# A planned attention and feed-forward kernel: later due times for some transfers, one operation that may change its engine, and the order drawn up anew

## The chip, the core and the metric

The kernel runs on one core of a Trainium2 chip. The core has TensorE (matrix products, results in PSUM), VectorE, ScalarE and GpSimd (elementwise work), and SyncE, which here issues every transfer. The engines run side by side, each through its own queue in order, and wait for one another by semaphores. The metric is the device time of one execution in microseconds (us); the median of several executions is compared. In the profile the engines are PE (matmuls), PEld (TensorE's weight loads), DVE (VectorE), ACT (ScalarE), POOL (GpSimd) and SP (SyncE); a q behind the name is the engine's sequencer.

## What is computed

```python
def _attn_ref(q, k, v):                      # (4, 8, 576, 64) each
    scores = scale * np.matmul(q, k.transpose(0, 1, 3, 2))
    mask = block_i >= block_j                # blocks of 64 positions
    scores = np.where(mask, scores, -1000000000.0)
    scores = scores - np.max(scores, axis=-1, keepdims=True)
    attn = np.exp(scores)
    attn = attn / (np.sum(attn, axis=-1, keepdims=True) + 1e-09)
    return np.matmul(attn, v)

def _moe_ref(x, w1, w2, w3, w_out):          # x: 2304 tokens x 512; w1, w2 512 x 1024, w3 1024 x 1024
    a = x @ w1
    b = x @ w2
    h = a * b @ w3
    return h @ w_out

def _moe2_ref(x, w_in, w_out):               # 512 x 2048, 2048 x 512
    h = x @ w_in
    g = np.where(h > 0.0, h, np.exp(np.minimum(h, 0.0)) - 1.0)
    return g @ w_out

# attention, then _moe_ref, then _moe2_ref
```

The weights arrive as 64-bit words, which the kernel turns into 32-bit floats on the chip.

## The kernel before

**Stages.** Attention is done for 16 pairs of heads (`attention`, n = 0 to 15). For a pair, q and k are loaded (lines 555; the first pair, `whole`, in two pieces each at line 550), copied to the matmul type by ScalarE with their remainders on GpSimd and VectorE (lines 591 to 604), then scores, row maxima on VectorE (lines 681, 748, 807), exponents on ScalarE (lines 686, 759, 819), transposes and the product with v (line 860). Beside the first pairs, weight blocks of 128 x 512 are converted (`convert`) and w3 is multiplied with w_out (`w_product`), so that the first feed-forward part needs one product less. `block2` runs that part over six blocks of 384 tokens, and the last stage (`part_h`, `part_o`) the second part, both with each operand split in two and three products per pair. In the second half of `block2`'s time the weights of the last stage are converted and combined (`t_unit`) and stored in DRAM, from which the last stage reads them again.

**A conversion.** `convert` issues a 512 KB load (line 471), then two ScalarE steps on the loaded words: `c0` (line 439, or on VectorE, line 441), which writes a `ct` buffer, and `c1` (line 432); VectorE steps `c2` to `c4` (lines 445, 448, 453), and the addition `c5` on GpSimd (lines 459, 462). The first conversions take turns in four raw slots (`raw64`, which lie in space that attention results use later) and three `ct` buffers. `w_product` ends with a copy on ScalarE and a subtraction on VectorE (lines 948, 951), which free its PSUM bank.

**Normalising.** When a pair's exponent sums are there, GpSimd adds them up (lines 893, 894), VectorE takes reciprocals (lines 886, 888), SyncE stores them to a scratch tensor in DRAM (line 901, four transfers) and fetches them back broadcast over partitions (line 909, three transfers of 144, 128 and 16 KB). Then GpSimd multiplies the pair's results with them in place (`norm`, line 921, 128 x 576). `block2` reads the results of four pairs.

**The order of work** is made by a planner when the kernel is built. `Plan.add` (line 196) takes each operation with an engine, an estimated duration, what it reads and writes, a priority, other engines it may run on (`ways`) and a `lag`. `Plan.run` (line 233) goes through estimated time: it takes the engine that can start an operation first and, of the operations that can start then, that of the lowest priority number, and emits it. So each engine's queue is fixed at build time. A transfer is estimated in lines 270 to 274: 1.8 us, its bytes at 300 GB/s behind the transfers before it, and 0.05 and 0.3 us; at most eight are in flight. An operation whose inputs end at a time is ready a little later (lines 286 and 287): by `SEEN` of its engine and by its own `lag`. Before the first product of `w_product` the planner also emits spare matmuls (line 1603) where it expects TensorE to be idle, so that TensorE doesn't stand still. `TURNS` (line 59) replaces the priority of single operations, by their number; it holds 520 entries.

```python
        o.prio = TURNS.get(o.n, o.prio)
...
                pipe = max(pipe, t + 1.8) + o.nbytes / 300e3 + 0.05
                o.end, free[e] = pipe + 0.3, t + 0.5
...
                    late = 0.0 if "GATE" in (e, u.eng) else self.SEEN[next(iter(u.ways))] + u.lag
                u.ready = max(u.ready, o.end + late)
```

Of the kernel before, what the change touches and what calls it, by code (L numbers as in the profile page):

```python
# [23 lines left out]
LAG = 0.1  # L24
NLEAD = 2
# [34 lines left out]
    5: -2499.99, 16: -2398.97, 29: -2498.05, 32: -2398.96, 47: -2398.96, 49: -2398.97, 51: -10090.89, 65: -2470.26,  # L60
    73: -2499.48, 83: -2499.91, 84: -9969.15, 90: -2499.99, 96: -2382.01, 99: -2536.18, 100: -10090.93, 105: -2486.89,
    110: -9965.2, 117: -2499.38, 118: -979.78, 120: -2495.46, 123: -2499.17, 138: -2499.41, 141: -2479.33,
    150: -2499.07, 157: -2497.98, 160: -2497.99, 164: -10051.79, 168: -10049.44, 169: -976.72, 173: -2498.88,
    177: -2497.99, 208: -2499.16, 210: -10117.81, 222: 40.01, 232: -10117.85, 248: -2546.58, 265: -2499.27,
    267: -2500.0, 273: -2498.28, 279: -2499.95, 281: -2494.99, 282: -2493.99, 286: -2498.69, 289: -10035.15,
    309: -2536.17, 313: -998.01, 333: -2491.66, 353: -10093.41, 358: -2493.99, 359: -2398.97, 363: -10093.4,
    370: -10025.68, 372: -10202.0, 379: -2498.88, 384: -10049.47, 385: -10117.8, 386: -10117.82, 387: -10117.84,
    394: -980.72, 401: -10074.7, 403: -9811.57, 411: -2393.99, 427: -10207.76, 444: -9971.65, 445: -9934.45,
    468: -991.98, 481: -2393.01, 503: -2435.46, 504: -2396.5, 505: -2394.01, 509: 10010.01, 525: -8999.99,
    532: -992.01, 533: -10066.53, 559: -991.99, 607: -991.99, 613: 44.01, 616: 45.97, 634: 46.01, 653: 54.01,  # L70
    672: -10024.51, 677: -2393.02, 678: -9000.03, 686: -2384.98, 689: -10000.01, 697: 42.02, 699: -2384.99,
    713: 79.99, 720: 498.18, 731: -10019.6, 744: -9928.04, 748: -9928.03, 755: -9881.69, 761: -9881.69, 763: 53.97,
    766: -10044.21, 768: -10008.85, 785: -2499.98, 803: 66.01, 804: -10001.91, 808: 65.99, 818: -10076.0, 819: 63.98,
    821: 64.51, 822: -10000.02, 823: 67.01, 848: 490.13, 876: -10272.6, 883: -10272.61, 887: -10160.95,
    889: -10160.94, 896: -10160.99, 898: -10160.96, 915: 8.35, 936: 118.77, 942: -10161.0, 951: 10121.63,
    954: -9963.56, 961: 509.01, 975: 112.01, 986: -10161.03, 989: 132.33, 997: -10176.58, 1004: -10176.57,
    1008: -10176.56, 1009: 104.0, 1011: -10161.05, 1014: -10018.92, 1017: -10189.77, 1019: -10161.02, 1024: -10176.6,
    1052: -9998.99, 1055: -10231.87, 1061: -10176.62, 1063: -10127.57, 1072: -10231.88, 1073: 152.94, 1078: 82.42,
    1088: 103.97, 1090: 103.97, 1116: 155.74, 1126: 184.21, 1136: -10017.39, 1147: -10017.4, 1154: -10176.62,
    1174: 55.0, 1175: -987.59, 1181: 54.99, 1184: 528.98, 1185: 101.83, 1194: -10022.9, 1203: 71.99, 1206: -10047.65,  # L80
    1209: 19.03, 1213: 505.99, 1218: 72.08, 1220: -10070.02, 1221: 505.01, 1225: -9968.26, 1232: 70.01,
    1233: -9875.34, 1240: 511.0, 1242: -9980.39, 1243: 84.99, 1274: -10032.31, 1275: 129.99, 1283: 132.0,
    1284: -9999.01, 1296: -10176.63, 1298: 156.1, 1347: 136.02, 1348: -9990.74, 1349: 126.99, 1357: 136.02,
    1360: 153.29, 1361: 151.47, 1369: -10157.37, 1371: -9880.0, 1407: 144.01, 1416: 142.1, 1424: 135.97,
    1429: -9999.02, 1431: 11456.16, 1433: 143.99, 1440: 135.94, 1442: 143.98, 1480: 155.01, 1484: -10069.46,
    1486: -10069.47, 1497: 151.99, 1498: 151.99, 1531: -10014.96, 1533: -10014.95, 1542: 10040.01, 1556: 10019.98,
    1557: 52.11, 1558: 10080.65, 1562: -9985.61, 1563: -10008.86, 1567: 61.96, 1569: 538.43, 1579: 10050.01,
    1586: 63.99, 1587: -10272.57, 1593: 65.96, 1595: -10161.02, 1596: -10160.96, 1601: 51.99, 1602: -9947.44,
    1606: -9881.7, 1607: -9985.6, 1608: 79.99, 1609: -9985.59, 1614: 10075.01, 1615: 65.98, 1628: -10160.99,
    1630: -10147.07, 1631: -10161.01, 1632: -10161.02, 1648: 505.02, 1650: -10047.64, 1655: -10161.01,  # L90
    1657: -10160.96, 1665: 92.12, 1666: -10176.57, 1670: -10176.57, 1673: -10176.57, 1674: -10176.58, 1679: 103.98,
    1680: 103.97, 1693: 109.38, 1694: -9789.98, 1695: -10176.63, 1698: -10176.59, 1699: -10176.61, 1701: -10176.6,
    1706: -10185.48, 1707: -10211.42, 1714: 11404.99, 1715: -9871.01, 1726: 142.4, 1727: 145.99, 1730: -9834.31,
    1731: 11410.02, 1732: 132.01, 1734: 103.93, 1738: 134.51, 1739: 125.98, 1741: 125.99, 1750: 144.02,
    1755: 12662.72, 1761: 12705.01, 1774: 100.86, 1780: 148.04, 1782: 143.99, 1783: 135.95, 1810: 12734.98,
# [1565 lines left out]
```

## Time and profile before

| | us |
|---|---|
| median of 3 runs | 903.3 |
| lowest and highest | 900.35, 904.62 |
| profiled execution, whole time | 904.66 |
| its span, first to last instruction | 902.9 |
| TensorE busy (matmuls) | 882.3 |
| VectorE, GpSimd, ScalarE busy | 720.0, 566.3, 505.0 |

The profile is of one execution. Its span is the time from the first to the last instruction; the whole time is 1.8 us longer. Busy means that an instruction of the engine is in flight. Matmuls overlap in TensorE's pipeline, so its busy time counts no time twice but says nothing on how full the pipeline is; its granted clock was 1.00 of full speed. A wait is put down to the instruction or transfer that came last before the waiting one began.

### The profile page before, as it was taken

Reading aid. Unit: us, or ns where it says so; the run is one execution under the profiler, and the core shown is the slowest. Engines: PE = TensorE matmul, PEld = TensorE weight load, DVE = VectorE, ACT = ScalarE, POOL = GpSimd, SP = SyncE. Lnnn points to the kernel's source line nnn. Section 1 sums busy time; section 2 is a strip of 40 time slices with the busy share of each in tenths; the row PEclk is TensorE's granted clock in tenths of the full one; section 3 lists DMA queues with packets and bytes.
Section 4 is the critical chain, followed back from the end, with each engine's and each line's share of the span. In section 5 each row is a group of like instructions: output and inputs, shape, how many; then the busy total and the mean of one; then the engine's idle time right before and its main releaser. Section 6 shows DMA issues by size and latency. Waiting matters only on the chain.

```text
span 902.9 us, 15289 instructions
## 1 busy us (share of the span) xinstructions
PE 882.3 (98%) x5233; PEld 784.3 (87%) x5233; DVE 720.0 (80%) x1349; ACT 505.0 (56%) x1151; POOL 566.3 (63%) x570
## 2 busy tenths in 40 slices
PE   8998999999999999999999999999999999999998
PEld 4544479787878789999999999999999999999998
DVE  6988898877656666668888887879897688887896
ACT  6866587776566654336354554446545465544461
POOL 3676677665423236579888884137876378951786
PEclk9999999999999999999999999999999999999999
DMA  6767643556422106777475967777589776788656
GB/s 223 234 174 226 204 142 108 162 162 190 139 78 77 58 15 225 227 238 254 163 246 198 313 202 250 249 233 250 206 285 309 252 264 208 237 325 276 227 185 232
DMA packets 101037, 186.14 MB, mean 206 GB/s; under 512 B 8544, under 2 KB 51040, under 8 KB 100960
## 3 DMA queue, kind: packets, MB, share of 16 engines
q1 hardware_dynamic: 100960, 185.18, 62.2%
q8 instruction: 41, 0.67, 0.3%
q14 instruction: 36, 0.29, 0.1%
HBM read 147.85 MB, written 37.30 MB: 205 GB/s over the span
## 4 chain that ended last, share of the span: by engine, by line
PE 74%; DVE 11%; DMA 7%; ACT 3%; POOL 3%; issue 2%; SPq 0%; POOLq 0%; DVEq 0%; ACTq 0%
PE y L1012 10%; PE b L1051 10%; PE a L1051 10%; PE hx L1302 7%; PE ox L1381 6%; PE oz L1381 5%; PE hz L1302 5%; PE hy L1302 4%; PE o L860 4%; PE oy L1381 3%; PE t L697 2%; DMA cr<-w 2%; PE s L658 2%; DMA out<-ob 2%; DVE ct L445 1%
## 5 line engine op out<-in xcount | busy, mean ns | idle before, releaser
L1012 PE MATMUL y<-g,slab_lo 128*128 128x384 f32 x576 | 114.9, 340 | 1.7 <-DVE xy L1035 1.0
L1051 PE MATMUL a<-xs,slab_lo 128*128 128x384 f32 x576 | 111.3, 337 | 0.0
L1051 PE MATMUL b<-xs,slab_lo 128*128 128x384 f32 x576 | 111.1, 337 | 0.0
L1012 PEld LDWEIGHTS y<-g,slab_lo 128*128 128x128 f32 x576 | 99.1, 188 | 4.5 <-DVE xy L1035 2.0
L1051 PEld LDWEIGHTS b<-xs,slab_lo 128*128 128x128 f32 x576 | 100.0, 188 | 0.9 <-DVE slab_lo L951 0.7
L1051 PEld LDWEIGHTS a<-xs,slab_lo 128*128 128x128 f32 x576 | 100.0, 188 | 0.9 <-DVE ct L453 0.4
L1302 PE MATMUL hx<-sy,win 128*128 128x384 f32 x432 | 86.6, 336 | 0.6 <-DVE ga L1184 0.5
L1302 PEld LDWEIGHTS hx<-sy,win 128*128 128x128 f32 x432 | 75.5, 188 | 2.2 <-DVE ga L1184 1.5
L1381 PE MATMUL ox<-sp,wout 128*128 128x384 f32 x372 | 74.2, 334 | 0.0
L973 POOL TENSOR_TENSOR g<-af,g 128x384 fp32r<-128x384 f32 x48 | 55.0, 1149 | 29.8 <-ACT g L970 29.3
L1381 PEld LDWEIGHTS ox<-sp,wout 128*128 128x128 f32 x372 | 65.4, 188 | 0.0
L937 PE MATMUL wps<-full,full 128*128 128x512 f32 x128 | 59.9, 602 | 3.2 <-POOL full L462 2.0
L439 ACT ACTIVATE ct<-cr 128x512 f32<-128x512 f32 x61 | 41.3, 677 | 33.2 <-POOL wt L462 16.0
L1302 PE MATMUL hz<-sy,win 128*128 128x384 f32 x288 | 58.1, 336 | 0.3
L1302 PE MATMUL hy<-sy,win 128*128 128x384 f32 x288 | 57.6, 335 | 0.8 <-DVE ga L1184 0.8
L432 ACT ACTIVATE cr<-cr 128x512 int32<-128x512 uint32 x72 | 48.8, 681 | 16.0 <-DMA cr<-w 9.0
L1175 POOL TENSOR_TENSOR sp<-ga,sp 128x384 fp32r<-128x384 f32 x23 | 25.3, 1107 | 49.8 <-ACT sp L1174 37.9
L860 PEld LDWEIGHTS o<-pt,v 128*64 128x64 f32 (+1 forms) x448 | 27.8, 135 | 31.8 <-issue 6.8
L860 PE MATMUL o<-pt,v 128*64 128x320 f32 (+4 forms) x448 | 52.7, 367 | 2.7 <-ACT pt L528 2.3
L921 POOL TENSOR_TENSOR xy<-xy,rr 128x576 f32<-128x576 f32 x16 | 23.3, 1454 | 48.6 <-DMA rr<-scr 29.9
L1381 PE MATMUL oz<-sp,wout 128*128 128x384 f32 x264 | 51.8, 336 | 1.4 <-DVE cp L1184 1.2
L459 POOL TENSOR_TENSOR ct<-ct,cr 128x512 int32<-128x512 int32 x28 | 39.9, 1426 | 20.5 <-DVE ct L453 10.8
(194 smaller groups left out, 2228.1 us busy)
## 6 DMA issues: line engine op xcount, KB each, us to landing
wout<-wso SPq DMA_DIRECT2D x84, 512.0 KB
cr<-w SPq DMA_DIRECT2D x48, 512.0 KB
win<-wsi SPq DMA_DIRECT2D x24, 1024.0 KB
win<-wsi SPq DMA_DIRECT2D x24, 768.0 KB
cr<-w3T SPq DMA_DIRECT2D x16, 512.0 KB
wsi<-wh SPq DMA_DIRECT2D x8, 896.0 KB
wsi<-wt SPq DMA_DIRECT2D x8, 896.0 KB
wso<-wh SPq DMA_DIRECT2D x8, 896.0 KB
```

The lines of the kernel that those rows point to most:

```text
L432: nc.scalar.activation(out=low, in_=low.bitcast(U32), func=AF.Copy, scale=2.0**-29)
L439: nc.scalar.activation(out=t().bitcast(F32), in_=words()[1].bitcast(F32), func=AF.Abs)
L459: nc.gpsimd.tensor_tensor(out=t(), in0=t(), in1=words()[0], op=ALU.add)
L860: nc.tensor.matmul(o()[D * h:D * h + D, lo:cols], lhsT=vt()[0:kn, j, D * h:D * h + D], rhs=p, start=(j == 0), stop=(j == last),)
L921: nc.gpsimd.tensor_tensor(out=a, in0=a, in1=rr(), op=ALU.mult)
L937: nc.tensor.matmul(ps(), lhsT=a[:, j, :], rhs=bb, start=(j == 0), stop=(j == KF - 1))
L973: lambda: nc.gpsimd.tensor_tensor(out=g()[:, 1, :], in0=src(), in1=g()[:, 0, :].bitcast(F32), op=ALU.subtract),
L1012: nc.tensor.matmul(ps()[:, 0:T2], lhsT=w[:, a, n * P:(n + 1) * P], rhs=gs[m]()[:, c, :], start=(m == ms[0] and q == 0), stop=(m == ms[-1] ...
L1051: nc.tensor.matmul(ps()[:, 0:T2], lhsT=w[:, a, u, k, :], rhs=xs()[:, k, c, :], start=(k == 0 and q == 0), stop=(k == KD - 1 and q == 2),)
L1175: lo = lambda eng: eng.tensor_tensor(out=dst(1), in0=src(), in1=dst(0).bitcast(F32), op=ALU.subtract)
L1302: nc.tensor.matmul(bk()[:, 0:T3], lhsT=w[:, a, k, :], rhs=s_(c), start=(first and k == 0 and i == 0), stop=(k == 1 and i == 2), skip_group ...
L1381: nc.tensor.matmul(to[n]()[:, 0:T3], lhsT=w[:, a, n * P:(n + 1) * P], rhs=sp(c), start=(first and q == 0 and i == 0), stop=(q == KP - 1 an ...
```

## The change

`LOADED` (0.5 us) becomes the `lag` of the two ScalarE steps of a conversion that read the loaded words, and of the ScalarE copies of q and k for all pairs but the first; the scaling of the first pair's k gets a lag of 0.7, and the normalisation one of `FETCH` (1.6 us). The normalisation may also run on VectorE, at an estimate of 0.76 us against 1.4 on GpSimd. `TURNS` is replaced: 447 entries stand where 520 stood, 146 operations have one in both, four of them with the same value. No operation is added or taken away, and no buffer changes.

```diff
 LAG = 0.1
+LOADED = 0.5
+FETCH = 1.6
...
 TURNS = {
-    5: -2499.99, 16: -2398.97, 29: -2498.05, 32: -2398.96, 47: -2398.96, 49: -2398.97, 51: -10090.89, 65: -2470.26,
...
+    5: -2499.99, 16: -2329.56, 17: -2495.99, 29: -2498.01, 32: -2329.57, 33: -10133.18, 35: -2499.98, 41: -2499.99,
...
         add(
-            "ACT", 0.68, lambda: c0(nc.scalar), r=[rk], w=[t], prio=prio,
+            "ACT", 0.68, lambda: c0(nc.scalar), r=[rk], w=[t], prio=prio, lag=LOADED,
             ways=[("DVE", 0.42, lambda: c0(nc.vector), True)],
         )
-        add("ACT", 0.68, c1, r=[rk], w=[rk2], prio=prio)
+        add("ACT", 0.68, c1, r=[rk], w=[rk2], prio=prio, lag=LOADED)
...
-                    "ACT", act_us(cn, True), lambda cs=cs: scale_k(nc.scalar, cs), r=[(ks, 0, c)], w=[(ks, 1, c)], prio=pr,
+                    "ACT", act_us(cn, True), lambda cs=cs: scale_k(nc.scalar, cs), r=[(ks, 0, c)], w=[(ks, 1, c)], prio=pr, lag=0.7,
...
-            add("ACT", 0.67, lambda: nc.scalar.copy(qs()[:, 0, :], raw()[:, 0, :]), r=[(raw, 0)], w=[(qs, 0)], prio=pr)
+            add("ACT", 0.67, lambda: nc.scalar.copy(qs()[:, 0, :], raw()[:, 0, :]), r=[(raw, 0)], w=[(qs, 0)], prio=pr, lag=LOADED)
...
-                r=[(raw, 1)], w=[(ks, 0)], prio=pr,
+                r=[(raw, 1)], w=[(ks, 0)], prio=pr, lag=LOADED,
...
-        def norm():
+        def norm(eng):
             a = xy[b]()[:, hp, :]
-            nc.gpsimd.tensor_tensor(out=a, in0=a, in1=rr(), op=ALU.mult)
+            eng.tensor_tensor(out=a, in0=a, in1=rr(), op=ALU.mult)
 
         add(
-            "POOL", 1.4, norm, r=[(rr, 0, 0), (rr, 1, 0), (rr, 1, 1), *((xy[b], hp, c) for c in range(2))],
-            w=[(xy[b], hp, "n"), *((xy[b], hp, c) for c in range(2))], prio=pr, port=True,
+            "POOL", 1.4, lambda: norm(nc.gpsimd), r=[(rr, 0, 0), (rr, 1, 0), (rr, 1, 1), *((xy[b], hp, c) for c in range(2))],
+            w=[(xy[b], hp, "n"), *((xy[b], hp, c) for c in range(2))], prio=pr, port=True, lag=FETCH,
+            ways=[("DVE", 0.76, lambda: norm(nc.vector), True)],
         )
```

## Rows read from the trace of the kernel before

**Rows 1.** The page's busy table: us busy, share of span, instructions

```profile
PE 882.3 (98%) x5233; PEld 784.3 (87%) x5233; DVE 720.0 (80%) x1349; ACT 505.0 (56%) x1151; POOL 566.3 (63%) x570
```

**Rows 2.** TensorE's timeline, start: start us, us, engine, line, out<-in, count [idle before]

```profile
1.96 2.31 PE L1603 MATMUL spare<-mk 128*128 128x512 bf16 x5 [1.96 <-POOL mk L1449]
```

**Rows 3.** Timeline of the end, TensorE's last matmuls

```profile
894.93 4.33 PE L1381 MATMUL oy<-sx,wout 128*128 128x384 f32 x24
```

**Rows 4.** Busy us by stretch: stretch, length, each engine (instructions), clock, DMA share, GB/s

```profile
core 0: us, PE busy (x) PEld busy (x) DVE busy (x) ACT busy (x) POOL busy (x), PEclk, DMA share, GB/s
0.00:125.00 125.00, 113.58 (x540) 60.44 (x540) 106.58 (x208) 85.44 (x199) 76.51 (x93) 1.00 0.66 208
125.00:350.00 225.00, 223.30 (x1583) 185.62 (x1584) 162.15 (x429) 147.12 (x406) 111.66 (x133) 1.00 0.36 115
350.00:850.00 500.00, 496.92 (x2838) 490.59 (x2837) 409.54 (x655) 250.00 (x500) 335.99 (x309) 1.00 0.74 247
```

**Rows 5.** TensorE's timeline, 0 to 125 us: matmuls that waited

```profile
51.29 0.87 PE L697 MATMUL t<-ident,p 128*128 128x128 f32 x6 [1.18 <-ACT p L686]
...
68.31 0.44 PE L770 MATMUL t<-ident,p 128*128 128x128 f32 x2 [1.04 <-DVE pt L529]
...
76.17 0.87 PE L860 MATMUL o<-pt,v 128*64 128x256 f32 x8 [1.77 <-ACT pt L528]
...
98.90 17.57 PE L937 MATMUL wps<-full,full 128*128 128x512 f32 x40 [1.15 <-DVE slab_lo L951]
```

**Rows 6.** TensorE's timeline, 205 to 245 us: matmuls that waited

```profile
215.97 1.86 PE L1012 MATMUL y<-g,slab_lo 128*128 128x384 f32 x9 [1.02 <-DVE xy L1035]
238.91 0.87 PE L860 MATMUL o<-pt,v 128*64 128x256 f32 x8 [0.33 <-DVE pt L529]
```

**Rows 7.** Chain of waits, 0 to 130 us: start us, us, what

```profile
50.27 6.16 DMA rr<-scr
...
59.37 3.05 DMA rr<-scr
...
89.25 6.34 DMA cr<-w
```

**Rows 8.** Chain of waits, 205 to 240 us: two loads

```profile
208.27 5.97 DMA cr<-w
...
232.16 4.71 DMA cr<-w
```

**Rows 9.** Timelines of ScalarE and VectorE, 46 to 101 us

```profile
48.64 0.43 DVE L441 TENSOR_SCALAR ct<-cr 128x512 int32<-128x512 int32 x1 [0.68 <-DMA cr<-w3T]
...
74.61 0.66 ACT L439 ACTIVATE ct<-cr 128x512 f32<-128x512 f32 x1 [2.51 <-POOL full L462]
...
95.67 0.66 ACT L439 ACTIVATE ct<-cr 128x512 f32<-128x512 f32 x1 [2.45 <-DMA cr<-w]
...
98.16 0.68 DVE L951 TENSOR_TENSOR slab_lo<-wps,slab_lo 128x512 fp32r<-128x512 f32 x1
```

**Rows 10.** GpSimd's timeline, 50 to 75 us

```profile
56.55 1.41 POOL L921 TENSOR_TENSOR xy<-xy,rr 128x576 f32<-128x576 f32 x1 [1.76 <-DMA rr<-scr]
...
62.58 1.40 POOL L921 TENSOR_TENSOR xy<-xy,rr 128x576 f32<-128x576 f32 x1 [1.35 <-DMA rr<-scr]
...
73.23 1.35 POOL L462 TENSOR_TENSOR full<-ct,cr 128x512 int32<-128x512 int32 x1 [0.41 <-issue]
```

**Rows 11.** Waits, 125 to 350 us: engine, line <- releaser: total us, times, longest

```profile
POOL xy L921 <- DMA rr<-scr: 26.8, 5, 7.7
```

**Rows 12.** Instruction groups, whole span: count | busy us, mean ns | idle before

```profile
L921 POOL TENSOR_TENSOR xy<-xy,rr 128x576 f32<-128x576 f32 x16 | 23.3, 1454 | 48.6 <-DMA rr<-scr 29.9 <-DVE st L807 7.9 <-ACT cr L432 4.4
...
L604 DVE SCALAR_TENSOR_TENSOR k<-raw,k 128x576 fp32r<-128x576 f32 x15 | 11.3, 754 | 0.1
```

**Rows 13.** Instruction groups of GpSimd, 0 to 125 us

```profile
L462 POOL TENSOR_TENSOR full<-ct,cr 128x512 int32<-128x512 int32 x24 | 31.8, 1324 | 23.5 <-ACT p L819 10.3 <-DVE ct L453 9.1 <-ACT cr L432 1.8
L459 POOL TENSOR_TENSOR ct<-ct,cr 128x512 int32<-128x512 int32 x9 | 13.3, 1479 | 3.0 <-DVE ct L453 2.3 <-ACT p L759 0.7
...
L921 POOL TENSOR_TENSOR xy<-xy,rr 128x576 f32<-128x576 f32 x4 | 5.6, 1407 | 8.8 <-ACT cr L432 4.4 <-DMA rr<-scr 3.1 <-DVE ct L453 1.3
```

138 rows, old and new, of the table TURNS are left out of this document.

## The prediction, made before the changed kernel ran

> **What bounds the kernel now.** I read the busy table first: over the 902.9 us span TensorE has work in flight for 882.3 us, VectorE for 720.0, GpSimd for 566.3, ScalarE for 505.0 [rows 1]. TensorE is the bound, so the only time that a new order can give back is TensorE's idle time, 902.9 - 882.3 = 20.6 us. Two pieces of it belong to no order: 1.96 us before the first matmul [rows 2] and 902.9 - (894.93 + 4.33) = 3.64 us after the last one, in which results are added and stored [rows 3]. That leaves 15.0 us. The view by stretches says where [rows 4]: 125.0 - 113.58 = 11.4 us in the first 125 us (9.5 without the start), 1.7 from 125 to 350, 3.1 from 350 to 850, the rest at the end. So the first stretch is the one to look at. In it VectorE is the second bound, 106.58 of 125 us.
>
> Third, the waits of TensorE in that stretch one by one [rows 5], and the two of the next stretch [rows 6]; then the chain of waits backwards from them. Two kinds of transfer stand in the chain: weight blocks that take 6.34, 5.97 and 4.71 us from issue to use [rows 7, 8], and the fetch of the reciprocal sums, 6.16 and 3.05 us [rows 7]. The plan in the code prices the first at 1.8 + 524288/300000 + 0.05 + 0.3 = 3.9 us (`run`, 512 KB), and the last fetch of a pair (16 KB) at 2.2 us. It orders each engine's queue by these prices, and the engines then execute in that order: an instruction that waits for a late transfer holds all that stands behind it.
>
> **Part 1, weights seen 0.5 us later (LOADED in `convert`).** No instruction is added. What can be gained are stalls in which TensorE stands behind an engine that stands behind a load. Four are to be seen. At 48.64 VectorE waited 0.68 us for a block [rows 9]; the maximum that stands behind it made ScalarE's exponent late, and TensorE waited 1.18 at 51.29 [rows 5]: worth 0.68. At 95.67 ScalarE had waited 2.45 us for a block; VectorE's next conversion steps had to wait for ScalarE, and the subtraction of line 951, which frees a PSUM bank, came behind them, at 98.16 [rows 9]; TensorE waited 1.15 at 98.90 [rows 5]. At 215.97 and 238.91 TensorE waited 1.02 and 0.33 [rows 6], each on VectorE, with a load of 5.97 and 4.71 us in the chain just before [rows 8]. Sum 0.68 + 1.15 + 1.02 + 0.33 = 3.18 us. The measured loads are 0.8 to 2.4 us later than the price, and the added 0.5 covers only a part; if a later place gained no more than the 0.5 itself, it would be 3 x 0.5 + 0.33 = 1.83 us. I take 3.2, since what a plan changes is which instruction stands first: once line 951 or the maximum stands ahead of the waiting step, its whole delay is gone. Bounds 1.8 and 3.2.
>
> The rows show loads of 4.71 to 6.34 us [rows 7, 8]. [...]
>
> **Part 2, reciprocal sums 1.6 us later (FETCH).** In the first stretch GpSimd stood idle 1.76 us at 56.55 and 1.35 us at 62.58 waiting for the fetch [rows 10], and both fetches are links of the chain [rows 7]. Queued behind the second on GpSimd are the sums of the next pair and the next conversions, down to the one at 73.23 [rows 10]; VectorE's reciprocal waits for the sums, the next blocks' first steps for the conversions' buffers, and TensorE waits 1.04 at 68.31 and 1.77 at 76.17 [rows 5], the last through ScalarE, which stood 2.51 us behind the conversion of 73.23 [rows 9]. 1.6 is under the slip of the first fetch (6.16 - 2.2 = 4.0) and over that of the second (0.8). I count the 1.04 whole and half of the 1.77, since the conversion of 73.23 had waited for something other than the fetch just before it [rows 10]: 1.9 us. Bounds: 0 (another wait is next) and 1.76 + 1.35 = 3.1. Four of the sixteen normalisations lie in the first 125 us [rows 13], the other twelve in the next stretch. There GpSimd waits 26.8 us for the fetch [rows 11], but TensorE idles 1.7 us in all that stretch [rows 4]: hidden, worth nothing.
>
> **Part 3, normalising on VectorE.** The operation is 1.454 us on GpSimd, x16 [rows 12]. VectorE has none; the nearest row is its 128x576 scalar_tensor_tensor with both tensors in SBUF, 0.754 us [rows 12]. The way is open, not forced: the plan takes whichever engine is free first. The four of the first 125 us, all on VectorE, would add 4 x 0.754 = 3.0 us to an engine that is 85% busy there, and take 5.8 from GpSimd, which is 61% busy. I put it at nothing: it is hidden in VectorE's own idle time, and if that cover is gone it costs up to 3.0; if instead GpSimd's place in the chain is what counts, it gains 4 x (1.454 - 0.754) = 2.8. Both ends stay.
>
> **Part 4, q, k and the first k piece.** ScalarE's copies of q and k see LOADED too; no stall that is shown [rows 5, 6] comes back to them: nothing. The first pair's k is seen 0.7 later. The plan fills expected idle time of TensorE at the start with spare matmuls, five in 2.31 us [rows 2], and may put one more there. One spare more is 2.31/5 = 0.46 us on the path at worst; I take 0.2, bounds 0 and 0.5.
>
> **Part 5, the order anew.** The table of turns is replaced nearly whole (520 entries by 447), so every stage is dealt again: the attention products among the weight products, the loads on SyncE's queue, the last stage. No row prices this. The remaining idle of TensorE is 15.0 - 3.2 - 2.8 = 9.0 us, and a new order can recover some of it or add as much. Value 0, bounds -4.5 (half of it) and +6 (the price of the slower rival below).
>
> **Sum.** -3.2 - 1.9 + 0 + 0.2 + 0 = -4.9 us. The profiled execution took 904.66 us, which gives 899.8; it stands 1.4 above the median of the runs shown (903.3, from 900.35 to 904.62), and on that median the forecast is 903.3 - 4.9 = **898.4 us**. With the bounds of parts 1 and 2 alone it runs from -1.8 + 0.2 to -3.2 - 3.1 + 0.2, so 897 to 902.
>
> **Rivals.**
> *Nothing that counts.* The lags cover stalls that come back elsewhere: 0.5 is a quarter of the worst slip (6.34 - 3.9 = 2.4), so the engine waits a little later on the same load, and VectorE, 85% busy in the first stretch [rows 4], becomes what TensorE waits for. It includes the case that no norm leaves GpSimd. For it: 26.8 of GpSimd's 29.9 us of waits on the fetch [rows 11, 12] are in the stretch where nothing depends on them. Against it: the stalls shown [rows 5, 6], each with a late transfer in its chain. Time 903 to 904.
> *Slower: conversions fall a turn behind.* In the first 125 us, 24 + 9 = 33 weight blocks [rows 13] pass through four raw slots, some 8 rounds, and each round needs its first step before the next load may be issued. If the plan puts another instruction in front of a step that is in truth ready, each round ends one VectorE step of 0.68 us later (line 951, [rows 9]), 33/4 x 0.68 = 5.6 us, and the products of the next stretch, which need these weights, start that much later: 903.3 + 5.6 = 908.9. It decides once loads land by the old price rather than by the measured one. For it: the stretch's conversions and VectorE are nearly full. Against it: the loads in the chain are all late by more than the lag.
> *A larger gain.* The new order also recovers half of the 9.0 us that is left: 898.4 - 4.5 = 893.9. For it: the idle is there; against it: 3.1 us of it is spread over 500 us of the later stretches [rows 4].
>
> **How the numbers follow.** Forecast case (897 to 902): 0.45, of which 0.27 falls below 898.8. Larger gain: 0.17. Nothing that counts: 0.18. Slower: 0.20. 0.5% is 4.5 us, about what a measurement of this kernel can tell from no change. Faster by more: 0.27 + 0.17 = 0.44. Within: 0.18 + 0.18 = 0.36. Slower by more: 0.20. The range runs from 892 to 908: below it lies a part of the larger gain (about 0.05), above it the upper half of the slower case (about 0.13). The forecast's own range is 897 to 902.
>
> **What would show it.** In the changed kernel's trace: TensorE's idle in 0 to 125 us falls from 11.4 to about 7 (parts 1, 2); GpSimd's two waits for the fetch before 100 us are gone or under 0.5; line 951 near the end of the weight products no longer stands behind a conversion that waited for a load; some of the sixteen normalisations are on VectorE, at 0.75 to 0.85 us each. It is wrong if the first stretch ends at the same idle with the waits moved to VectorE, or if the stretch from 350 on changes by more than 3 us, which would make part 5 the largest term.

## The result and the profile after

The changed kernel takes 895.3 us (median, 892.2 to 898.7), the kernel before, measured beside it, 904.6 (900.4 to 909.1). The ratio is 0.990, with a 95% interval of 0.987 to 0.993: 9.3 us faster. The forecast was 4.9 us faster; the result lies inside the range (892 to 908), below the forecast's own part of it (897 to 902), and beside the rival called a larger gain (893.9). The profiled execution took 893.4 us, span 891.3, against 904.66 and 902.9.

The lines of the changed kernel's code stand 9 or 10 lower than those of before. Its busy table, against [rows 1]:

```profile
PE 875.9 (98%) x5233; PEld 783.3 (88%) x5233; DVE 717.4 (80%) x1375; ACT 504.0 (57%) x1143; POOL 546.1 (61%) x552
```

TensorE's idle time fell from 20.6 to 891.3 - 875.9 = 15.4 us, so by 5.2 us; its busy time fell too, by 6.4 us, though it runs the same 5233 instructions. More than half of the profile's gain lies inside what the table calls busy. The view by stretches, against [rows 4]:

```profile
0.00:125.00 125.00, 116.84 (x583) 64.52 (x584) 109.20 (x221) 95.98 (x220) 82.19 (x99) 1.00 0.68 213
125.00:350.00 225.00, 223.76 (x1582) 187.08 (x1581) 167.53 (x429) 138.87 (x386) 103.40 (x126) 1.00 0.36 117
350.00:850.00 500.00, 497.94 (x2860) 495.06 (x2859) 411.43 (x686) 252.41 (x503) 328.51 (x302) 1.00 0.74 249
```

In the first 125 us TensorE idles 8.2 us instead of 11.4, but it has also begun 583 matmuls there instead of 540. Equal stretches of time don't hold equal work. Its waits of 0.3 us and more in that stretch, the 1.96 us before the first matmul aside:

```profile
13.96 0.66 PE L687 MATMUL t<-ident,p 128*128 128x128 f32 x4 [0.46 <-ACT p L676]
17.41 0.61 PE L715 MATMUL s<-k,q 64*128 64x256 f32 x6 [1.50 <-ACT p L676]
20.84 1.13 PE L928 MATMUL wps<-full,full 128*128 128x512 f32 x2 [1.05 <-POOL full L452]
23.56 0.44 PE L760 MATMUL t<-ident,p 128*128 128x128 f32 x2 [0.60 <-DVE pt L519]
51.45 1.12 PE L928 MATMUL wps<-full,full 128*128 128x512 f32 x2 [0.35 <-POOL full L452]
56.82 0.66 PE L687 MATMUL t<-ident,p 128*128 128x128 f32 x4 [0.48 <-ACT xy L518]
86.38 25.99 PE L928 MATMUL wps<-full,full 128*128 128x512 f32 x60 [1.55 <-POOL full L452]
```

[Rows 5] shows four of the nine such waits of the kernel before. The others are 0.75 us at 15.05, 1.12 at 21.25, 0.60 at 30.33, 0.57 at 40.70 and this one:

```profile
72.56 0.66 PE L770 MATMUL t<-ident,p 128*128 128x128 f32 x4 [0.51 <-DVE xy L529]
```

Up to 45 us the two kernels wait about alike, 3.04 us before and 3.61 after. From 45 to 125 us the kernel before waits 5.14 us in the four stalls of [rows 5] and 0.51 in this one, 5.65 in all; the changed kernel waits 0.35, 0.48 and 1.55, so 2.38 us. The start, the fetch and the normalisations, against [rows 2, 11, 12]:

```profile
1.96 2.74 PE L1594 MATMUL spare<-mk 128*128 128x512 bf16 x6 [1.96 <-POOL mk L1440]
...
POOL xy L911 <- DMA rr<-scr: 5.9, 1, 5.9
...
L911 POOL TENSOR_TENSOR xy<-xy,rr x10: 1396/1427/1949, 47.4 to 325.4; 128x576 f32<-128x576 f32 x10
L911 DVE TENSOR_TENSOR xy<-xy,rr x6: 747/754/1132, 190.1 to 337.7; 128x576 f32<-128x576 f32 x6
```

Six spare matmuls stand at the start instead of five. GpSimd waits for a fetch of sums once in 125 to 350 us, 5.9 us instead of 26.8, and not at all before. Six of the sixteen normalisations run on VectorE (0.754 us), the first at 190.1 us; the early ones all stay on GpSimd. The weight loads in the chain take 5.47 to 6.73 us, so they are as late as before [rows 7, 8]:

```profile
43.67 6.61 DMA cr<-w3T
61.28 5.74 DMA cr<-w3T
77.81 5.91 DMA cr<-w3T
163.98 5.47 DMA cr<-w
221.19 6.73 DMA cr<-w
```

The changed kernel's longest stall of that stretch, 1.55 us at 86.38, still comes from one of them, the load of 77.81. ScalarE waited for it, VectorE and GpSimd for ScalarE, and TensorE for GpSimd's result:

```profile
83.81 0.67 ACT L429 ACTIVATE ct<-cr 128x512 f32<-128x512 f32 x1 [2.38 <-DMA cr<-w3T]
```

The subtraction that frees a PSUM bank (now line 942) still stands on VectorE behind such a conversion step, at 85.54, but it is not what TensorE waits for there.

**Loss by work done.** To compare kernels stage by stage I gave each of TensorE's matmuls its usual step, the median distance to the next start for its line and shape in the kernel before (173 ns for the 128 x 384 ones). The sum of the steps so far is the work done, 852 us in all, the same in both kernels. The time of a matmul's start less the work done by then is the loss up to there. It sees short waits that the busy time hides: a matmul of that shape is some 334 ns in flight, so a wait of up to 161 ns between two starts leaves no idle time. From here on this table is used, in us, one profiled execution of each kernel:

```
                    loss when so much work is done          loss within
work done, us         125     225     550     850      225 to 550  550 to 850
before               20.4    29.9    39.6    46.7          9.7        7.1
after                14.6    23.0    33.0    35.3         10.0        2.3
early_new            13.7    22.4    56.8    65.4         34.5        8.6
early_old            22.9    32.9    56.4    60.3         23.5        3.9
e_front              21.2    30.3    39.8    48.7          9.6        8.8
e_last               19.3    28.4    38.0    45.1          9.6        7.2
lags_old_turns       21.7    33.1    49.4    58.2         16.3        8.8
new_turns_no_lags    18.6    33.9    47.2    50.8         13.3        3.6
n_pool               15.9    26.1    36.0    39.8          9.9        3.8
m_all                21.3    31.7    41.4    48.5          9.7        7.1
s_old_new            21.5    30.9    41.7    45.3         10.8        3.5
x_assign             18.4    28.3    39.8    55.6         11.5       15.7
half_before          14.8    22.7    32.4    39.0          9.7        6.6
half_after           13.5    20.2    30.1    34.3          9.9        4.1
```

The changed kernel is 6.9 us ahead at 225 us of work (attention and the weight products), no further at 550, and gains another 4.8 us in the last stage, which none of the new due times and no normalisation touches. Executions of one order differ: where the first half is in before's order or nearly so (before, early_old, e_last, m_all, s_old_new, x_assign), the loss at 225 runs from 28.3 to 32.9; with the new order (after, early_new, n_pool) from 22.4 to 26.1. So a single profile is good to some 2 us either way, and the two groups don't touch. Part of the spread is TensorE's clock. In stretches of 20 us the granted clock was 0.74 in lags_old_turns and 0.91 in new_turns_no_lags (both 40 to 60 us), 0.91 in early_old (60 to 80) and s_old_new (0 to 20), 0.97 and 0.94 in m_all (80 to 120), and 0.83 in early_new (520 to 560) and early_old (540 to 560); all other stretches ran at 1.00. In lags_old_turns that is at most (1 - 0.74) x 20 = 5.2 us of its loss.

### The profile page after: what moved, and what is told of

Read it like the earlier page. It is cut to its first block, busy times and chain, and to the rows that moved or that the text cites. A ratio compares the mean times of both kernels' runs of the same rounds, so it can differ in the third digit from the quotient of the medians.

```text
span 891.3 us, 15293 instructions
## 1 busy us (share of the span) xinstructions
PE 875.9 (98%) x5233; PEld 783.3 (88%) x5233; DVE 717.4 (80%) x1375; ACT 504.0 (57%) x1143; POOL 546.1 (61%) x552
## 4 chain that ended last, share of the span: by engine, by line
PE 82%; DVE 7%; DMA 4%; ACT 2%; issue 2%; POOL 2%; SPq 1%; POOLq 0%; DVEq 0%; ACTq 0%
PE b L1042 10%; PE a L1042 10%; PE y L1003 10%; PE hx L1293 8%; PE ox L1372 8%; PE oz L1372 6%; PE hy L1293 5%; PE hz L1293 5%; PE oy L1372 5%; PE o L850 3%; PE wps L928 3%; PE t L687 2%; DMA cr<-w3T 2%; PE s L648 2%; DMA cr<-w 1%
## 5 line engine op out<-in xcount | busy, mean ns | idle before, releaser
L1166 POOL TENSOR_TENSOR sp<-sum,sp 128x384 fp32r<-128x384 f32 x30 | 32.5, 1087 | 45.0 <-ACT sp L1165 45.0
L429 ACT ACTIVATE ct<-cr 128x512 f32<-128x512 f32 x58 | 39.4, 678 | 25.1 <-POOL wt L452 15.7
L1372 PE MATMUL oy<-sp,wout 128*128 128x384 f32 x252 | 51.8, 334 | 0.0
```

Of the source, the lines that this page charges most:

```text
L429: nc.scalar.activation(out=t().bitcast(F32), in_=words()[1].bitcast(F32), func=AF.Abs)
L1166: lo = lambda eng: eng.tensor_tensor(out=dst(1), in0=src(), in1=dst(0).bitcast(F32), op=ALU.subtract)
L1372: nc.tensor.matmul(to[n]()[:, 0:T3], lhsT=w[:, a, n * P:(n + 1) * P], rhs=sp(c), start=(first and q == 0 and i == 0), stop=(q == KP - 1 an ...
```

## The experiments

All experiment kernels hold both tables of turns (their lines stand 135 to 149 higher than in the kernel before). `made(turns, lags, way)` lists the order that the planner makes with one table, with or without the new due times, and with or without VectorE for the normalisation: a row [operation, engine, place, spare matmuls] for each operation. OLD is (TURNS_OLD, False, False), NEW is (TURNS, True, True). The rows are then issued by place, each when what it depends on has been issued. `made(*OLD)` gives before, `made(*NEW)` gives after. `MARK["late"]` is the number of the first operation of the late conversions and the last stage.

### Half of each order: early_new, early_old, s_old_new

```diff
-        return made(*NEW)
+        return mix(made(*NEW), made(*OLD), lambda n: n < MARK["late"])    # early_new; early_old swaps the two plans
+        ...                                                               # s_old_new: one seam in time
+        x, y = made(*OLD), made(*NEW)
+        pe = [r for r in x if r[1] == "PE"]
+        cut = pe[700][2]
+        iy = index(y)
+        return [r if r[2] < cut else [r[0], iy[r[0].n][1], 1e6 + iy[r[0].n][2], iy[r[0].n][3]] for r in x]
```

> Both tables of turns are kept in the kernel. Attention, weight products and the second half's weight work are ordered as in the changed kernel; the conversions that run late and the whole last stage are ordered as before. Split theory (the gain is about 6.5 us in the work up to the first 225 us of TensorE's work and about 5 us in the last stage): 904.6 - 6.5 = about 898, the stretch from 350 us on as in the kernel before. Theory of transfers (parts 1 and 2 of the prediction and what goes with them are the whole gain): about 895, as the changed kernel. If the gain is only the last stage's: 904 to 905.

> The reverse: everything up to the last stage ordered as before, with every norm on GpSimd and the old due times; the late conversions and the last stage ordered as in the changed kernel. Split theory: 904.6 - 5 = about 899.7, with TensorE's idle time of the first 125 us still at 11.4 us and its late steps in the last stage (32 steps that came more than 25 ns late, 7.0 us in all, before; 8 steps, 2.2 us, after) as in the changed kernel. Theory of transfers: no change, 904 to 905, since the late loads and the fetches of the reciprocal sums lie in the first part.

Measured: early_new 923.5 us (ratio to before 1.023, 1.020 to 1.026), early_old 913.3 (1.012, 1.009 to 1.015). By total time every theory failed. The table shows where: two orders interleaved by operation lose 34.5 and 23.5 us where they meet, between 225 and 550 us of work. At most 6.8 and 3.4 us of that are the stretches at the lower clock. That a conversion of the one order and the buffer it needs in the other come at different places would explain the rest, but it was not traced. On either side of the seam the halves did what the split theory says: early_new's loss at 225 is 22.4, as in after; its last stage loses 8.6, as in the other old orders; early_old is the reverse, 32.9 and 3.9.

> The order of before up to the point at which the last stage has just begun (there both orders have issued the same set of instructions, so the seam costs nothing), and the changed kernel's order from there on. If the table of turns is worth 4 to 5 us in the last stage by itself, the time falls by that, to 899.5 to 900.5, with TensorE's late steps after 550 us at 2 to 4 us in all instead of 7. If the last stage's gain needs the earlier first half: 903 to 905.

Here one seam in time does no harm: 900.2 us, ratio 0.996 (0.994 to 0.998), 3.1 us faster, and the last stage loses 3.5 instead of 7.1. So the last stage's gain comes from that stage's new order, in which the engines chosen and the order of matmuls and loads are new too, and it needs nothing of the first half. It is smaller than the 4.8 that one pair of profiles gave: old orders lose 6.6 to 8.8 us there, new ones 2.3 to 4.1, in the table's rows other than x_assign. By the medians 9.3 - 3.1 = 6.2 us are left for the first half.

### Are late transfers what the first half loses? half_before, half_after

```diff
-        add("SP", 0, lambda: nc.sync.dma_start(out=like(rawt(), src), in_=src), w=[rk, rk2], ...)
+        def load():
+            d = like(rawt(), src)
+            if u < 8 or not first:
+                nc.sync.dma_start(out=d, in_=src)
+            elif len(src.shape) == 3:
+                nc.sync.dma_start(out=d[:, :1], in_=src[:, :1])
+            else:
+                nc.sync.dma_start(out=d[:, :HS // 2], in_=src[:, :HS // 2])
+        add("SP", 0, load, w=[rk, rk2], ...)
```

> The order of before; of the weight blocks converted in the first half, all after the eighth are loaded by half (256 KB instead of 512 KB; the other half of the block is left over from an earlier one, so part of the weights is left out). If late transfers are what the first half loses (parts 1 and 2 of the prediction), TensorE reaches the first 225 us of its work 4 to 7 us earlier and the time falls to 898 to 901. If the conversions' own work on VectorE, ScalarE and GpSimd is what it waits for, the gain is under 2 us.

> The same halved loads in the changed kernel's order. If the new order gains by going round late loads, it has less left to win: 1 to 3 us below the changed kernel's 895, and the two orders come closer in the first half (their distance of 6.9 us at 225 us of TensorE's work falls under 4). If the order's gain has nothing to do with the loads, the distance stays at 6 to 7.

Measured: half_before 896.5 us (0.992, 0.989 to 0.995), half_after 891.9 (0.987, 0.984 to 0.990). Beside 903.3 for before in the same measurement, before's order gains 6.8 us from lighter loads; the new order gains 895.3 - 891.9 = 3.4 (from two measurements; by the two ratios 2.7). At 225 us of work the two orders are 29.9 - 23.0 = 6.9 us apart with whole loads and 22.7 - 20.2 = 2.5 with halved ones. By the medians it is 9.3 us for the whole loads and 896.5 - 891.9 = 4.6 for the halved ones, again 4.7 less. So 4 to 5 us of the 6.9 is the new order's way round late transfers, and some 2.5 (about the spread of one profile) is something else. The queues of half_before hold the order of before. Its time fell below the 898 to 901 expected; the first half's 7.2 us (29.9 - 22.7) are just above the 4 to 7 expected, and the distance of 2.5 is under the 4. TensorE's waits of 0.4 us and more in half_before from 45 to 125 us, its first stretch, its waits for weight blocks and three halved loads in its chain:

```profile
50.42 0.88 PE L841 MATMUL t<-ident,p 128*128 128x128 f32 x6 [0.41 <-ACT p L830]
72.24 0.87 PE L1004 MATMUL o<-pt,v 128*64 128x256 f32 x8 [0.63 <-ACT pt L672]
...
0.00:125.00 125.00, 118.18 (x576) 65.28 (x576) 111.36 (x219) 90.52 (x212) 81.00 (x96) 1.00 0.51 152
...
ACT ct L574 <- DMA cr<-w: 2.3, 4, 0.9
...
47.98 2.20 DMA cr<-w3T
...
65.60 4.98 DMA cr<-w3T
...
225.19 3.72 DMA cr<-w
```

Of the four stalls of [rows 5], 1.18 became 0.41, 1.77 became 0.63, and 1.04 and 1.15 are gone, as is the 0.51. The stretch's idle time fell by 4.6 us. GpSimd no longer waits for the first two fetches [rows 10] either, so this run doesn't tell the weights' share from the sums': they share SyncE's queue. ScalarE's waits for w blocks on this line, up to 350 us, went from 7.7 us in the kernel before to 2.3. With the other line and the w3T blocks ScalarE waited 19.4 us for weight blocks in the kernel before, 9.1 here and 11.2 in the changed kernel: the new order waits less for loads that come as late as ever. The halved loads took 2.20 to 4.98 us, the whole ones of the changed kernel's chain 5.47 to 6.73.

### Can the stalls be mended by hand? e_front, m_all, e_last

```diff
-        return made(*OLD)
+        p = made(*OLD)
 ...                                                   # e_front
+        norm = sorted(n for n in at if ix[n][0].lag == FETCH)
+        pool = [r[0].n for r in p if r[1] == "POOL"]
+        ix[norm[0]][2] = at[pool[pool.index(norm[1]) - 1]] + 0.5
+        ix[norm[1]][2] = at[399] + 0.5
+        for n, before in ((162, 370), (416, 518)):
+            ix[n][2] = at[before] - 0.5
 ...                                                   # e_last
+        for n, before in ((2814, 2808), (3022, 2852), (3077, 3228), (3097, 3082), (3337, 3149), (4035, 4220)):
+            ix[n][2] = at[before] - 0.5
 ...                                                   # m_all, for each row r whose operation o has a new lag
+                due = max(d.end for d in o.deps if engine[d.n] == "SP") + self.SEEN[next(iter(o.ways))] + o.lag
+                if r[4] < due:
+                    r[2] = next((i for i, t in enumerate(ts) if t >= due and i > r[2]), len(ts)) - 0.5
```

Here `ix` gives an operation's row and `at` its place in the old order.

> The order of before with four instructions moved, all in the first 125 us: the first two normalisations go behind one conversion each on GpSimd (the ones that started at 59.74 and 65.63), the maximum goes ahead of the conversion step that waited 0.68 us for its block at 48.64, and the subtraction of line 951 goes ahead of the conversion step that it stood behind at 98.16. The prediction's parts 1 and 2 give 0.68 + 1.15 of weights and 1.0 to 1.9 of the fetches: 2.8 to 3.7 us faster, about 901.4. The rival (the stall is only handed on to the next late thing) gives 0 to 0.5 us.

> The order of before, in which only those instructions are moved that the new due times would hold back, each behind the work that the plan has ready in the time added (0.5, 1.6 and 0.7 us). On the engines this moves one conversion step by one place in two places on VectorE, and on GpSimd one early normalisation behind a conversion and some later ones behind one instruction. The prediction's parts 1 and 2 give 898.4 + 1.4 = about 900 if such moves are the gain. The theory after the hand-moved orders (a stall is handed on to the next late thing): 903 to 905, no change.

Measured: e_front 906.6 us (1.003, 1.001 to 1.005), slower by 0.3%; m_all 904.5 (0.999, 0.998 to 1.001), no change. In e_front three of the four moves took place; the subtraction stayed, since what it needs is issued later. TensorE's waits there, against [rows 5]:

```profile
48.73 1.12 PE L1082 MATMUL wps<-full,full 128*128 128x512 f32 x2 [1.12 <-POOL full L606]
64.76 0.79 PE L802 MATMUL s<-k,q 64*128 64x384 f32 x5 [0.76 <-ACT p L903]
70.76 0.44 PE L914 MATMUL t<-ident,p 128*128 128x128 f32 x2 [2.75 <-DVE pt L673]
99.41 17.77 PE L1082 MATMUL wps<-full,full 128*128 128x512 f32 x40 [0.61 <-DVE slab_lo L1096]
```

The stall of 51.29 (1.18) went, and one of 1.12 came 2.6 us earlier, on a conversion's result. GpSimd's first two fetch waits went (a later norm, at 97.68, then waits 4.09 us), and with them the stalls of 68.31 and 76.17, but in their place stand 0.76 and 2.75. The wait of 0.51 stayed (0.52 at 75.00). The stalls are handed on, as the rival said. In part the moves themselves did that: VectorE's casts of the two normalised results were moved back only as far as the norms, and now hold up what stands behind them on VectorE by 2.61 and 2.02 us, where they had waited 0.75 and 0.84 before:

```profile
61.42 0.36 DVE L1133 CAST xs<-xy 128x384 fp32r<-128x384 f32 x1 [2.61 <-POOL xy L1065]
...
68.49 0.36 DVE L1133 CAST xs<-xy 128x384 fp32r<-128x384 f32 x1 [2.02 <-POOL xy L1065]
```

So e_front shows that these moves are worth nothing; moves that put the casts further back, too, were not tried. m_all applies the due times alone: they change the order of before at few places, and those are worth nothing.

> The order of before with six instructions moved, all after 600 us: six evacuations of a PSUM bank on VectorE, each put ahead of the one VectorE instruction that it stood behind while TensorE waited (stalls of 0.66 at 607.1, 0.61 at 634.5, 0.24 at 651.9, 0.36 at 657.5, 0.40 at 692.9 and 0.97 at 866.5). If the last stage's gain comes from which instruction stands ahead of an evacuation, these stalls go and the time falls by up to their sum, 3.2 us, to 901.4. If the stalls only move to the next bank, 0 to 0.5 us.

Measured: 903.8 us (1.000, 0.997 to 1.002), no change, and the last stage loses 7.2 us as before. All six moves took place, and no other instruction changed its place. TensorE's waits of 0.2 us and more in the last stage, of the kernel before:

```profile
607.10 1.33 PE L1302 MATMUL hx<-sy,win 128*128 128x384 f32 x6 [0.50 <-DVE ga L1184]
634.46 1.31 PE L1381 MATMUL oz<-sp,wout 128*128 128x384 f32 x6 [0.44 <-DVE cp L1184]
692.94 1.31 PE L1381 MATMUL oz<-sp,wout 128*128 128x384 f32 x6 [0.24 <-DVE ob L1184]
753.68 2.89 PE L1381 MATMUL oz<-sp,wout 128*128 128x384 f32 x15 [0.71 <-DVE cp L1184]
866.54 1.33 PE L1302 MATMUL hy<-sy,win 128*128 128x384 f32 x6 [0.81 <-DVE ga L1184]
```

of e_last, in part:

```profile
591.64 1.30 PE L1443 MATMUL hz<-sy,win 128*128 128x384 f32 x6 [0.53 <-DMA win<-wsi]
634.61 2.20 PE L1522 MATMUL oz<-sp,wout 128*128 128x384 f32 x11 [0.34 <-DVE sp L1316]
649.88 0.61 PE L1522 MATMUL oz<-sp,wout 128*128 128x384 f32 x2 [0.42 <-DVE sp L1316]
...
880.80 2.35 PE L1522 MATMUL ox<-sx,wout 128*128 128x384 f32 x12 [0.49 <-DMA wout<-wso]
```

and of the changed kernel:

```profile
742.11 2.37 PE L1372 MATMUL oz<-sp,wout 128*128 128x384 f32 x12 [0.49 <-DVE cp L1175]
884.48 3.36 PE L1372 MATMUL oy<-sx,wout 128*128 128x384 f32 x18 [0.51 <-DMA wout<-wso]
```

607 and 866 are gone in e_last, and 649.88, 591.64 and 880.80 are new. Not all of that is the moves' doing: 591.64 lies ahead of the first moved instruction (at 604 us), and it and 880.80 wait for loads, whose queue is that of before. How a stall is handed on is seen on VectorE at 632 us, where one evacuation was put ahead of the first of these instructions, first before, then e_last:

```profile
632.53 1.41 DVE L1267 SCALAR_TENSOR_TENSOR gb<-gb,ga 128x384 f32<-128x384 f32 x1
...
634.33 2.17 DVE L1175 TENSOR_TENSOR sp<-gb,sp 128x384 fp32r<-128x384 f32 x2
```

```profile
631.42 0.55 DVE L1408 SCALAR_TENSOR_TENSOR gb<-gb,ga 128x384 f32<-128x384 f32 x1
631.89 2.66 DVE L1316 TENSOR_TENSOR sp<-gb,sp 128x384 fp32r<-128x384 f32 x2
```

The same instruction takes 1.41 us in one order and 0.55 in the other, and the next two take 2.17 and 2.66 us for both, so 0.49 of the 0.86 us comes back. TensorE no longer waits 0.44 us for the evacuation but 0.34 for one of these two. VectorE's instructions with all inputs in SBUF can be stretched while GpSimd is at work. In the kernel before, from 548 us on, 174 of its two-input instructions on 384 columns read SBUF alone: the 54 that overlap no instruction of GpSimd take at most 0.56 us, and of the 120 that do, 88 take over 0.62, up to 1.42. The 256 with an input in PSUM take at most 0.57, though 180 of them overlap one. The Trainium skill, "SBUF — State Buffer", section "Who interferes with whom", says that the two share a port pair under an exclusive lock, and these counts agree in the main (32 of the 120 were not stretched).

### Order or choice of engine? x_assign

```diff
-        return made(*OLD)
+        eng = {r[0].n: r[1] for r in made(*NEW)}
+        return [[o, eng[o.n] if o.n >= MARK["late"] else e, k, f] for o, e, k, f, _ in made(*OLD)]
```

> The order of before, TensorE's and the transfers' queues unchanged; only in the late conversions and the last stage each elementwise instruction runs on the engine that the changed kernel gives it (124 go from GpSimd to VectorE, 111 back, 17 from ScalarE to VectorE, 12 back), at its old place in the order. If the choice of engine is what makes the last stage faster: 899 to 901. If it is the order together with the choice: 904 or slower.

Measured: 914.7 us, ratio 1.012 (1.009 to 1.015). The last stage loses 15.7 us. Engine choice without its order is worse than either kernel. It also speaks against the simplest reading of the last stage, that the new order gains by fewer collisions on the port: summed over VectorE's elementwise instructions of over 0.62 us after 548 us, the time above 0.55 us is 46.4 us in before, 34.6 in after, 35.7 in s_old_new and 35.8 in x_assign, which stalls most. Two of its new stalls:

```profile
622.75 0.62 PE L1518 MATMUL ox<-sp,wout 128*128 128x384 f32 x2 [0.65 <-DVE sp L1312]
624.15 1.31 PE L1439 MATMUL hx<-sy,win 128*128 128x384 f32 x6 [0.78 <-DVE ga L1321]
```

Here TensorE waits for a remainder of an operand (sp), too, and no longer for evacuations alone; it also waits for loads, 0.60 us at 557.80 and 0.86 at 593.80. That fits a loss that depends on what stands ahead of the instruction that TensorE waits for, and not on how much VectorE has to do, but the run doesn't show it.

### Due times or table? lags_old_turns, new_turns_no_lags

```diff
-        return made(*NEW)
+        return made(TURNS_OLD, True, True)    # lags_old_turns
+        return made(TURNS, False, True)       # new_turns_no_lags
```

> The new due times and the way to VectorE, with the old table of turns. If the due times themselves bring the gain of the first half (parts 1 and 2 of the prediction), the first 225 us of TensorE's work end 3 to 7 us earlier than before: about 898 to 901. If the table of turns is what brings it and the old table only fits the prices it was made with, the order is no better or worse than before: 904 to 912.

> The new table of turns with the old due times (weights, q, k and the sums priced as before; the way to VectorE stays). If the due times bring the first half's gain, this loses it: 900 to 902, with the last stage as in the changed kernel. If the table brings it by itself: 895 to 897. If the two only fit together: over 904, the loss in the first half.

Measured: lags_old_turns 912.7 us (1.007, 1.005 to 1.009), new_turns_no_lags 907.3 (1.003, 1.000 to 1.005). Neither half of the change is faster than before. At 225 us of work they lose 33.1 and 33.9, where the order of before loses 28.3 to 32.9 and the new one 22.4 to 26.1. The profile of lags_old_turns took 916.6 us and holds the stretch at a clock of 0.74; without it its loss would be 28 at the least, so within the spread of before's order. What it loses beyond that comes later, 16.3 us from 225 to 550 where before loses 9.7. The new table keeps its gain in the last stage without the due times (3.6); with the old table the due times bring none there (8.8). So neither brings the first half's gain alone, in the one order that each gave. The longest wait of each, first the new table with the old due times:

```profile
55.05 0.67 PE L931 MATMUL s<-k,qb 128*128 128x288 f32 x3 [2.60 <-ACT p L821]
```

Then the old table with the new due times:

```profile
561.20 1.34 PE L1438 MATMUL hx<-sy,win 128*128 128x384 f32 x6 [1.47 <-DVE ga L1320]
```

The first is a wait for ScalarE's exponent, the second one for an evacuation where the last stage begins; the changed kernel waits at neither place.

### The normalisation back on GpSimd: n_pool

```diff
-        return made(*NEW)
+        return [[o, "POOL" if o.lag == FETCH else e, k, f] for o, e, k, f, _ in made(*NEW)]
```

> The changed kernel's order, with the six normalisations that it puts on VectorE (all after 188 us) back on GpSimd at the same place in the order. Part 3 of the prediction (worth nothing): 895 to 896, within 1 us of the changed kernel. If the place on VectorE is worth its 0.7 us each, or if GpSimd's wait for the sums now holds work that TensorE needs: 898 to 900.

Measured: 896.5 us, ratio 0.990 (0.986 to 0.994), the changed kernel's own ratio. The way to VectorE is worth nothing that can be measured; four executions, with an interval of 0.4% either way, would not show a difference of 2 or 3 us.

## Why the prediction was right, and where it was wrong

**Direction and size.** Faster was right. The sum, -4.9 us, was about half of the -9.3, and most of what was missing is the last stage.

**What bounds the kernel.** The premise that only TensorE's idle time, 15.0 us, could be given back failed. The busy share hides every wait shorter than the time for which a matmul is in flight beyond its step. Idle time fell by 5.2 us in the profile, the span by 11.6, so 6.4 us came from what the premise called busy. Reading the distance between matmul starts, and not their busy time, would have shown 39.6 + 7.1 = 46.7 us of loss in before, 7.1 of it in the last stage, where the view by stretches had 3.1 us for 350 to 850.

**Part 1, weights (-3.2), and part 2, sums (-1.9).** The mechanism was right: late transfers cost the first half 7.2 us (29.9 - 22.7, half_before), and the new order's way round them is worth 4 to 5 us against the 5.1 of the two parts. The four stalls of [rows 5] were the right ones; they are those that shrink when the loads are halved, by 4.1 us, and of the two of [rows 6] nothing of 0.3 us is left there; in the changed kernel's stretch from 125 to 350 us the longest wait is 0.70. The two parts weren't told apart. What failed is the reason given for each stall's price: "once line 951 or the maximum stands ahead of the waiting step, its whole delay is gone". In e_front the maximum did stand ahead and both norms were out of the way, and the time did not fall. These stalls were not terms that a move could strike out one by one; what gained was an order drawn anew, with its table. So the agreement of 4 to 5 us with 5.1 is in part luck: the stalls were the right ones, and each one's price stood on a rule that e_front contradicts. Nor did LOADED and FETCH bring the gain by themselves: m_all and lags_old_turns have them and gain nothing. The slips, too, are upper bounds: 3.9 us is the plan's price of a load with no transfer ahead of it, and the plan adds those ahead; no run shows how late the loads were against the plan's own times.

**Part 3 (0).** Right, and for a reason nearer than the one given: no norm of the first 125 us went to VectorE, and n_pool shows no difference within its interval.

**Part 4 (+0.2).** One spare matmul more at the start was right, 2.74 - 2.31 = 0.43 us of it; both kernels have eleven in all. It is not seen in the loss at 125 us.

**Part 5 (0, from -4.5 to +6).** This is the term that was mis-sized. In the last stage the order alone is worth 3.1 us by the medians (s_old_new) and some 4 by the table of losses, and a further part of the first half's 6.9 is left over from the loads (about 2.5, near the spread). The prediction said that a change of over 3 us from 350 us on would make part 5 the largest term; in equal windows it is hardly seen (idle 3.1 to 2.1 us), in equal work it is 4.8. So by that sign the account failed, though the time lies inside the range: the late transfers and the last stage's order gained about as much each. Its bound of half the idle time left, -4.5, was set by the failed premise, and the 9.0 us that it halves take off 2.8, part 3's outer bound, where part 2's 1.9 belongs; that would be 9.9.

**The rivals.** *Nothing that counts* was right about the moves tried (e_front, m_all) and wrong about the order as a whole. *Conversions a turn behind* did not come in the changed kernel; orders whose due times and table don't fit (lags_old_turns, early_new) do end later than before, by 7.9 and 19.5 us. *A larger gain* had the size and the right part, but looked for it in idle time.

**What stays open.** Why the new order of the last stage stalls less: single evacuations (e_last), the engines chosen (x_assign) and the total of port collisions were each ruled out as the cause by itself; the order as a whole does it. The new order of that stage is new in the queues of TensorE and of the loads, too; neither was tried by itself, nor the new order on the old engines. How the first half's gain divides between weights and sums was not separated.

## What to carry to other kernels

Measure an engine's loss by the distance between its starts against the usual step, by equal work and not by equal time: of the 47 us lost before, only 20.6 - 3.6 = 17 stood as idle time ahead of the last matmul's end, and a busy share of 98% hid the other 30. This planned order was one piece: due times, table and engine choice were each worth nothing or less by themselves for the whole time, so price such a change by what the late transfers cost as a whole (halve the loads and see), not by striking out stalls. An edit that says it concerns transfers but draws every queue anew must be priced in the stages it does not name, too.

## What was unexpected of the hardware

When two orders were spliced badly, TensorE's clock fell. Stretches of early_new, columns as in [rows 4]:

```profile
520.00:525.00 5.00, 1.29 (x8) 0.97 (x6) 1.30 (x3) 1.24 (x3) 1.81 (x3) 0.93 0.94 296
525.00:530.00 5.00, 4.79 (x15) 4.79 (x16) 0.84 (x2) 0.67 (x2) 1.00 (x1) 0.50 0.38 135
```

After a stretch in which TensorE was busy 1.29 of 5 us, the next one ran at a granted clock of 0.50, the lower of its levels (1.2 GHz), though it was busy for 4.79 us. lags_old_turns shows the same early on, after a stretch (35 to 40 us) in which TensorE was busy 3.33 of 5 us:

```profile
40.00:45.00 5.00, 3.68 (x23) 3.02 (x25) 4.59 (x12) 3.06 (x10) 3.22 (x5) 0.51 0.59 174
45.00:50.00 5.00, 5.00 (x21) 2.26 (x20) 3.18 (x7) 2.88 (x11) 2.22 (x3) 0.50 0.46 159
```

A gap so costs its own length and some of what follows: by an estimate from these rows, half of 4.79 us, so 2.4, in early_new, and up to 5 in lags_old_turns.
